# Products with v once per pair of heads, and one block fewer of the batch after next

## The chip, the cores and the metric

The kernel runs on one core of a Trainium2 chip. The metric is the device time of one execution in microseconds (us). "Faster", "same" and "slower" are said of the kernel after against the kernel before.

## What is computed

Eight batches of attention with a sigmoid in the place of the softmax, then a two-layer network over all tokens. Cut to what matters:

```python
batch, n_heads, seq, head_dim = (8, 12, 448, 64)
scores = scale * np.matmul(q, k.transpose(0, 1, 3, 2)) - np.log(S)
attn = 1.0 / (1.0 + np.exp(-scores))
x = np.matmul(attn, v)                  # -> [8*448, 768]
h = x @ w_in                            # 768 -> 2048
g = h - np.tanh(h)
out = g @ w_out                         # 2048 -> 768
```

## The kernel before

**The whole.** TensorE (PE in the profile) has by far the most work, and the order of its instructions is written out by hand: one instruction stream in which the network of batch b and the attention of later batches are interleaved. For each batch there are two stages. `moe1` computes `h` (tile `ph`, line L671) from the attention output `x`, which is split into a high and a low float16 half (`xhl`, L620 and L621), and then `g`. `moe2` computes the output: three tiles of 128 tokens (`po0` and `po1`, L789), each in 16 *steps* of 6 products, so 48 steps, and then a remainder of 64 tokens (`por`, L827), 16 shorter steps that count half. A position in a stage is thus a number from 1 to 56, and positions 16, 32 and 48 are the ends of the three tiles.

**The blocks.** Into the `moe2` stage of batch b the generator `stream` puts the attention of later batches, in *blocks*. A pair of heads takes two blocks. The first one (`i == 0`) transposes q of the next pair (`qT`, L298), the second one (`i == 1`) transposes k of the pair after (`kT`, L298 and L315). Both then compute the scores of two of the four key chunks of the pair (`sc`, L361, twelve products). ScalarE (ACT) makes the sigmoid (`a`, L370) and the high half of its result (`ahl`, L376), and VectorE (DVE) the low half (L377). These go to the list `todo`. `do_av` multiplies what the list holds with v (`acc`, L385, six products per chunk), always one block later than the scores, and with the fourth chunk the result goes out to `x` (L405, L414). In the second block of a pair ACT also reads k, q and v of a later pair for their norms (`sqn`, L307), and DVE makes the parts of k (`K`, L338 and L339).

**Where the blocks stand.** `BLOCKS0`, `BLOCKS1` and `BLOCKS` list the positions in the stages of batch 0, batch 1 and the others; this text calls them stage 0, stage 1 and so on. `ALONE` says after how many blocks of a stage the next batch is complete; what follows in the list belongs to the batch after it. Three positions after the last block that the next batch needs come its norms (`nm`, L598), and two and four positions later the rest of its `xhl`. Stage 6 runs the list only up to `ALONE`, and stage 7 has no blocks.

**Buffers.** `po0`, `po1` and `por` share two PSUM buffers (tag `mm`). At the end of a tile ACT copies `po0` out (`o`, L818) and DVE `po1` (`o`, L819); the next tile or `por` starts when its buffer is free. `qT` and `kT` share one PSUM buffer (`tr`), which `Q` and `K` on DVE set free (L339). ACT and DVE work in the order in which the program issues their instructions.

Of the kernel before, what the change touches and what calls it, by code (L numbers as in the profile page):

```python
# [34 lines left out]
class Builder:  # L35
# [6 lines left out]

    BLOCKS = (8, 12, 16, 20, 24, 28, 32, 36, 40, 44, 48, 52)
    TAIL = (1, 2, 3, 4, 5)
    ALONE = 8
    BLOCKS0 = (2, 5, 8, 12, 16, 20, 24, 31, 38)
    BLOCKS1 = (4, 7, 10, 13, 16, 19, 22, 25, 28, 32, 36, 40, 44, 48, 52)

    TP = 8
    SHIFT = 4  # L50
# [375 lines left out]
    def stream(self):  # L426

        NP = self.NP
        G = (self.B - 1) * NP
        at = lambda g: (1 + g // NP, g % NP)
        splits = lambda g: at(g)[0] >= self.AV32
        qk, v, ss, sc, K, Q, vv = {}, {}, {}, {}, {}, {}, {}

        def load(g):
            if g < G:
                qk[g] = self.load_qk(*at(g))
                if splits(g):  # L440
                    v[g] = self.load_v(*at(g), self.nat, "vn", 2)

        def norms(g):
            if g < G:
                ss[g] = self.norms(qk[g] + ([v[g]] if splits(g) else []))

        def turn(g, n, name):
            return self.transpose(qk[g][n], name) if g < G else None

        def turn_k(g):  # L450
            if g >= G:
                return None
            t = self.ps.tile([P, 512], F32, name="kT", tag="tr", bufs=1)
            turned = self.transpose(qk[g][0], "kT", t=t)
            sc[g] = self.scales(ss.pop(g), t)
            return turned

        def parts_k(g, t):
            if g < G:
                K[g] = self.parts(t, sc[g][0][:, 0:1], "K", not splits(g) and g not in (2, 3))  # L460

        def parts_q(g, t):
            if g < G:
                Q[g] = self.parts(t, sc[g][0][:, 1:2], "Q", True)
                qk.pop(g)

        def prep_v(g):
            if g >= G:
                return
            if splits(g):  # L470
                vv[g] = self.prep_v(v.pop(g), sc[g][0])
            else:
                vv[g] = self.load_v(*at(g), self.att, "vhl", 3)

        load(0)
        load(1)
        yield 0, False
        norms(0)
        norms(1)
        yield 0, False  # L480
        for g in range(2):
            parts_k(g, turn_k(g))
            yield 450, False
            parts_q(g, turn(g, 1, "qT"))
            load(g + 2)
            yield 450, False
        norms(2)
        norms(3)
        yield 0, False
        todo = []  # L490

        def do_av():
            for g, c, A in todo:
                if c == 0:
                    self.acc = self.ps.tile([P, 512], F32, name="acc", tag="av", bufs=1)
                    if g % NP == 0:
                        self.xs = []
                (self.av if splits(g) else self.av32)(c, self.acc, vv[g], A)
                if c == 3:
                    self.xs.append(self.evac_x(g % NP, self.acc, sc[g][1][:, 1:2] if splits(g) else None))  # L500
                    for d in (sc, K, Q, vv):
                        d.pop(g)
            todo.clear()

        for g in range(G):
            for i in range(2):
                if i:
                    t = turn_k(g + 2)
                elif g:
                    t = turn(g + 1, 1, "qT")  # L510
                pss = [self.scores(c, K[g], Q[g]) for c in (2 * i, 2 * i + 1)]
                aa = [self.weigh(pss[0], sc[g][1][:CK, 0:1])]
                if i:
                    parts_k(g + 2, t)
                elif g:
                    parts_q(g + 1, t)
                aa.append(self.weigh(pss[1], sc[g][1][:CK, 0:1]))
                do_av()
                if i == 0:
                    if g == 0:  # L520
                        prep_v(0)
                    prep_v(g + 1)
                if splits(g):
                    aa = [self.split_a(a) for a in aa]
                todo.extend((g, 2 * i + n, a) for n, a in enumerate(aa))
                if g and i == 0:
                    load(g + 3)
                elif g:
                    norms(g + 3)
                yield 2750, True  # L530
        do_av()
        yield 1150, True
# [344 lines left out]
    def first(self, rest):  # L877
# [17 lines left out]
        next(rest)  # L895
        assert n + len(self.BLOCKS0) + len(self.BLOCKS1) == 4 * self.NP + len(self.BLOCKS) - self.ALONE
        split = self.split_w_in()
# [14 lines left out]
    def batch(self, b):  # L912
# [12 lines left out]
        else:  # L925
            blocks = self.BLOCKS if b + 2 < self.B else self.BLOCKS[: self.ALONE + 1]
        alone = self.ALONE
        if b == 1:
            alone += len(self.BLOCKS1) - len(self.BLOCKS)
            blocks = self.BLOCKS1  # L930
        self.second(b, blocks, alone, events)
# [51 lines left out]
```

## Time and profile before

| what | us |
|---|---|
| runs of the kernel before, median of 3 | 1264.49 (1264.09 to 1266.74) |
| the profiled execution, its own time | 1264.9 |
| its span in the profile | 1262.7 |
| PE busy in it | 1234.1 |
| ScalarE busy | 933.0 |
| VectorE busy | 953.0 |

The span is what lies between the first and the last instruction; the 2.2 us beside it lie around the program. Times in rows are counted from the span's start. A row of a timeline gives the start, the length, the engine, the line, the operation, the tiles (out<-in), the shapes, the count of instructions that follow each other, and in brackets the idle time of the engine before them with what ended it.

### The profile page before, as it was taken

To read this page: it belongs to the slowest core of one execution; us is meant where nothing else is said; L and a number is where in the kernel's file an instruction comes from. 1 tells how busy PE (TensorE), PEld (TensorE's weight loads), DVE (VectorE), ACT (ScalarE), POOL (GpSimd) and SP (SyncE) were. 2 spreads that over 40 slices of the span, in tenths; PEclk is the share of its full clock that TensorE was granted. 3 is DMA by queue.
4 is the path that set the end of the run, shared out by engine and by line. 5 is a ranking of instruction groups with operands and counts; after the bars stand their busy time and mean duration, and the time that the engine had idled before them with its cause. 6 is when DMAs were issued, how large, how long until landed. Compare 5 with 4: busy or idle time off the path is not lost.

```text
span 1262.7 us, 20448 instructions
## 1 busy us (share of the span) xinstructions
PE 1234.1 (98%) x8011; PEld 683.9 (54%) x8011; DVE 953.0 (75%) x1488; ACT 933.0 (74%) x1311; POOL 37.9 (3%) x38
## 2 busy tenths in 40 slices
PE   8999879999999999999999999999999999999998
PEld 3245435555555555665555655555556655555555
DVE  4999988889876797676965798667976769645930
ACT  5967767958998688886878688886888868753820
POOL 0100000000010000100000000000000000000000
PEclk9999999999999999999999999999999999999999
DMA  9953254100122101220022200221012200100001
GB/s 258 294 139 84 58 156 138 43 27 1 36 73 57 42 2 42 65 65 7 1 57 64 56 1 16 64 58 41 1 43 67 62 7 1 28 14 20 1 13 32
DMA packets 114367, 70.52 MB, mean 56 GB/s; under 512 B 91872, under 2 KB 104416, under 8 KB 114272
## 3 DMA queue, kind: packets, MB, share of 16 engines
q1 hardware_dynamic: 114272, 69.23, 20.5%
q8 instruction: 63, 1.03, 0.3%
q14 instruction: 32, 0.26, 0.1%
HBM read 58.20 MB, written 11.01 MB: 55 GB/s over the span
## 4 chain that ended last, share of the span: by engine, by line
PE 76%; DVE 16%; ACT 4%; issue 3%; DMA 1%; SPq 0%; DVEq 0%; ACTq 0%
PE ph L671 30%; PE po L789 26%; PE sc L361 6%; PE acc L385 5%; PE por L827 3%; DVE ahl L377 2%; DVE xhl L621 2%; PE acc L395 2%; ACT a L370 1%; PE qT L298 1%; DVE sta L151 1%; DVE xhl L620 1%; DVE stb L151 1%; PE kT L298 1%; DVE wi L154 1%
## 5 line engine op out<-in xcount | busy, mean ns | idle before, releaser
L789 PE MATMUL po<-wo,g 128*128 128x384 f16 x2304 | 391.4, 326 | 1.0 <-ACT o L818 1.0
L671 PE MATMUL ph<-xhl,wi 128*128 128x448 f16 x2016 | 382.6, 352 | 0.0
L789 PEld LDWEIGHTS <-g 128*128 128x128 f16 x2304 | 219.5, 98 | 172.9 <-issue 32.4
L671 PEld LDWEIGHTS <-wi 128*128 128x128 f16 x2016 | 196.7, 98 | 185.0 <-issue 1.8
L370 ACT ACTIVATE a<-sc,nls,rn 112x896 f32<-112x896 f32 x168 | 179.7, 1094 | 45.8 <-PE sc L361 38.6
L377 DVE SCALAR_TENSOR_TENSOR ahl<-a,ahl 112x896 f16<-112x896 f32 x144 | 155.6, 1121 | 58.0 <-ACT ahl L376 57.2
L737 ACT ACTIVATE u<-ph,ih 128x896 f32<-128x896 f32 x64 | 64.4, 1006 | 99.0 <-PE ph L671 95.4
L376 ACT ACTIVATE ahl<-a 112x896 f16<-112x896 f32 x144 | 128.0, 939 | 0.0
L361 PE MATMUL sc<-Q,K 64*112 64x448 f16 x1008 | 115.2, 360 | 2.5 <-ACT a L370 2.5
L741 DVE SCALAR_TENSOR_TENSOR m<-ph,ihk,u 128x896 f32<-128x896 f32 x64 | 73.5, 1148 | 55.0 <-ACT th L739 54.7
L385 PE MATMUL acc<-ahl,vhl 112*64 112x448 f16 x864 | 96.4, 357 | 0.5
L655 ACT ACTIVATE g<-m,Sg 128x896 f16<-128x896 f32 x64 | 66.7, 1041 | 33.8 <-DVE m L755 28.7
L755 DVE COPY_PREDICATED m<-u,th 128x896 f32<-128x896 uint32 x64 | 77.1, 1205 | 6.6
L656 DVE SCALAR_TENSOR_TENSOR g<-m,Sg,g 128x896 f16<-128x896 f32 x64 | 73.4, 1147 | 8.3 <-ACT g L655 8.2
L339 DVE SCALAR_TENSOR_TENSOR Q<-qT,sn,Q 128x448 f16<-128x448 f32 x42 | 28.6, 682 | 66.8 <-ACT Q L336 66.7
L361 PEld LDWEIGHTS <-K 64*112 64x112 f16 x1008 | 59.6, 127 | 31.1 <-issue 5.2
L752 DVE SCALAR_TENSOR_TENSOR m<-q,m 128x896 f32<-128x896 f32 x64 | 69.9, 1093 | 7.4 <-DVE m L748 0.5
L701 PE MATMUL ph<-x,wi 128*128 128x448 f32 x192 | 75.1, 540 | 0.0
L742 DVE SCALAR_TENSOR_TENSOR th<-ph,ih,th 128x896 f32<-128x896 f32 x64 | 73.3, 1145 | 0.0
L754 ACT ACTIVATE u<-u,b 128x896 f32<-128x896 f32 x64 | 66.7, 1043 | 5.3 <-DVE m L741 3.3
L748 DVE SCALAR_TENSOR_TENSOR m<-q,m 128x896 f32<-128x896 f32 x64 | 69.6, 1087 | 0.0
L385 PEld LDWEIGHTS <-vhl 112*64 112x64 f16 x864 | 43.4, 109 | 47.8 <-issue 26.1
(134 smaller groups left out, 1321.7 us busy)
## 6 DMA issues: line engine op xcount, KB each, us to landing
raw<-moe_w_in SPq DMA_DIRECT2D x24, 512.0 KB, 6.0
rawo<-moe_w_out SPq DMA_DIRECT2D x32, 384.0 KB, 3.9
kn<-k SPq DMA_DIRECT2D x96, 112.0 KB, 2.9
qn<-q SPq DMA_DIRECT2D x96, 112.0 KB, 2.9
vn<-v SPq DMA_DIRECT2D x48, 224.0 KB, 2.6
out<-o SPq DMA_DIRECT2D x7, 336.0 KB, 3.3
out<-o SPq DMA_DIRECT2D x7, 288.0 KB, 3.1
out<-o SPq DMA_DIRECT2D x7, 240.0 KB, 2.6
```

The source lines that it names most:

```text
L361: nc.tensor.matmul(ps[:CK, h, :S], K[r, w, cs], Q[r, x, :], start=(n == 0), stop=(n == len(prods) - 1))
L370: nc.scalar.activation(a, ps[:CK, :, :S], AF.Sigmoid, bias=self.nls[:CK], scale=scale)
L376: nc.scalar.activation(A[:, 0], a, AF.Copy, scale=A_SCALE)
L377: nc.vector.scalar_tensor_tensor(A[:, 1], a, A_SCALE, A[:, 0], op0=ALU.mult, op1=ALU.subtract)
L385: nc.tensor.matmul(acc[h * D : (h + 1) * D, : self.S], v[:, w, h, c, :], A[:, x, h], start=(c == 0 and n == 0), stop=(c == 3 and n == 2),)
L656: nc.vector.scalar_tensor_tensor(g[:, 1], m, Sg, g[:, 0], op0=ALU.mult, op1=ALU.subtract)
L671: nc.tensor.matmul(ph[:, e, :S], self.wi[:, c * self.NB + k, part, e * P : (e + 1) * P], xhl[c][:, x, :], start=(i == 0), stop=(i == 3 * s ...
L701: nc.tensor.matmul(ph[:, e, :S], self.where("in", c)[:, f * P : (f + 1) * P], xs[c], start=(c == 0), stop=(c == self.NC - 1),)
L741: V.scalar_tensor_tensor(m, ps, ihk, u, op0=ALU.mult, op1=ALU.mult)
L742: V.scalar_tensor_tensor(th, ps, ih, th, op0=ALU.mult, op1=ALU.subtract)
L755: V.copy_predicated(m, u.bitcast(U32), th)
L789: nc.tensor.matmul(po[i][:, :H], gs[f // 2][:, x, f % 2, tk * P : (tk + 1) * P], self.wo[:, i * self.NF + f, w], start=(f == 0 and n == 0) ...
```

## The change

```diff
     TAIL = (1, 2, 3, 4, 5)
-    ALONE = 8
+    ALONE = 9
     BLOCKS0 = (2, 5, 8, 12, 16, 20, 24, 31, 38)
-    BLOCKS1 = (4, 7, 10, 13, 16, 19, 22, 25, 28, 32, 36, 40, 44, 48, 52)
+    BLOCKS1 = (4, 7, 10, 13, 16, 19, 22, 25, 28, 32, 36, 40, 46, 52)
@@ in stream
                 aa.append(self.weigh(pss[1], sc[g][1][:CK, 0:1]))
-                do_av()
+                if i == 0 or not splits(g):
+                    do_av()
```

For the pairs of batches 2 to 7 (`splits(g)`) the second block of a pair no longer multiplies with v; the first block of the next pair then does all four chunks, 24 products in place of 12. Batch 1 is as before. `ALONE` and the shorter `BLOCKS1` move one block: stage 1 has 14 blocks, not 15, and stages 2 to 5 still have 12 each, but begin one block earlier in the sequence (with the second block of pair 1, not the first of pair 2), so that every position holds the other kind of block. The last block that the next batch needs stands at position 44 there, not 40. Stage 6 has one block more. No instruction is added or left out.

On PE in stage 1, in the block at position 4 (a second block of its pair), before:

```order
L361 LDWEIGHTS K
L361 MATMUL sc<-Q,K 112x448
L385 LDWEIGHTS vhl
L385 MATMUL acc<-ahl,vhl 64x448
L385 LDWEIGHTS vhl
L385 MATMUL acc<-ahl,vhl 64x448
```

and in the changed kernel, where the line numbers below `do_av` are one higher:

```order
L361 LDWEIGHTS K
L361 MATMUL sc<-Q,K 112x448
L790 LDWEIGHTS g
L790 MATMUL po_3050<-wo,g 128x384
L790 LDWEIGHTS g
L790 MATMUL po_3051<-wo,g 128x384
```

The scores are now followed by the products of `moe2` at once; the products with v stand in the next block.

On PE at position 48 of stage 1, where the third tile ends, before:

```order
L789 MATMUL po_3889<-wo,g 128x384
L298 MATMUL qT<-ident,qn 128x112 x4
L361 LDWEIGHTS K
L361 MATMUL sc<-Q,K 112x448
L361 LDWEIGHTS K
```

and in the changed kernel:

```order
L790 MATMUL po_3888<-wo,g 128x384
L790 LDWEIGHTS g
L790 MATMUL po_3889<-wo,g 128x384
L828 LDWEIGHTS g
L828 MATMUL por<-wo,g 64x384
```

A block stood between the third tile and `por`; now `por` follows the tile directly, and the last block before it stands at position 46.

On ACT around that place the changed kernel has this order:

```order
L317 ACTIVATE tn<-kT,tiny 128x3
L370 ACTIVATE a_4153<-sc,nls,rn 112x896
L370 ACTIVATE a_4158<-sc,nls,rn 112x896
L376 ACTIVATE ahl<-a_4153 112x896
L376 ACTIVATE ahl<-a_4158 112x896
L307 ACTIVATE sqn,ss<-kn 112x512
L307 ACTIVATE sqn,ss<-qn 112x512
L307 ACTIVATE sqn,ss<-vn 112x512
L819 ACTIVATE o<-po_3888,iK 128x384
```

The copy `o` of `po0`, whose buffer `por` takes, stands behind all ACT work of the block just before it. These nine stood in the same order before, with two more steps of `moe2` between the block and the copy.

## Rows read from the trace of the kernel before

**Rows 1.** The page: busy us (share of the span) and instructions by engine.

```profile
PE 1234.1 (98%) x8011; PEld 683.9 (54%) x8011; DVE 953.0 (75%) x1488; ACT 933.0 (74%) x1311; POOL 37.9 (3%) x38
```

**Rows 2.** The timeline of PE over one block (`i == 1`) of stage 2.

```profile
493.05 0.55 PE L298 MATMUL kT<-ident,kn 112*128 112x112 f32 x4
...
493.66 1.34 PE L361 MATMUL sc<-Q,K 64*112 64x448 f16 x12
494.94 1.32 PE L385 MATMUL acc<-ahl,vhl 112*64 112x448 f16 x12
496.19 4.07 PE L789 MATMUL po<-wo,g 128*128 128x384 f16 x24
```

**Rows 3.** The chain that ended last: start, length, what; two `moe1`, batches 2 and 3.

```profile
423.91 54.59 PE ph L671 x288
...
570.94 54.59 PE ph L671 x288
```

**Rows 4.** The timeline of the end of stage 2, PE and DVE.

```profile
558.30 1.33 PE L385 MATMUL acc<-ahl,vhl 112*64 112x448 f16 x12
...
559.46 4.07 PE L827 MATMUL por<-wo,g 128*64 128x384 f16 x48
...
561.34 0.69 DVE L621 SCALAR_TENSOR_TENSOR xhl<-x,Sx,xhl 128x448 f16<-128x448 f32 x1
...
565.41 1.63 PE L385 MATMUL acc<-ahl,vhl 112*64 112x448 f16 x12
```

**Rows 5.** The timeline at the first block of stage 1 (position 4).

```profile
324.72 0.55 PE L298 MATMUL kT<-ident,kn 112*128 112x112 f32 x4
...
326.61 1.32 PE L385 MATMUL acc<-ahl,vhl 112*64 112x448 f16 x12
...
331.15 0.68 DVE L339 SCALAR_TENSOR_TENSOR K<-kT,sn,K 128x448 f16<-128x448 f32 x1
...
331.94 0.57 PE L298 MATMUL qT<-ident,qn 112*128 112x112 f32 x4 [0.98 <-ACT sqn L307]
```

**Rows 6.** The timeline at position 16 of stage 1, end of a tile.

```profile
352.17 0.60 DVE L819 TENSOR_SCALAR o<-po,iK 128x384 f32<-128x384 f32 x1
...
353.07 3.10 PE L789 MATMUL po<-wo,g 128*128 128x384 f16 x18
```

**Rows 7.** The timeline of ACT over one block (`i == 1`) of stage 1.

```profile
373.98 0.55 PE L298 MATMUL kT<-ident,kn 112*128 112x112 f32 x4
...
375.41 2.09 ACT L370 ACTIVATE a<-sc,nls,rn 112x896 f32<-112x896 f32 x2 [0.45 <-PE sc L361]
...
380.81 0.19 ACT L307 ACTIVATION_READ_ACCUMULATOR sqn<-vn 112x1 f32 x1
...
381.07 0.58 ACT L818 ACTIVATE o<-po,iK 128x384 f32<-128x384 f32 x1
```

**Rows 8.** The timeline of PE around its two longest pauses.

```profile
153.03 0.78 PE L361 MATMUL sc<-Q,K 64*112 64x448 f16 x6 [2.47 <-ACT a L370]
153.73 0.66 PE L298 MATMUL kT<-ident,kn 112*128 112x112 f32 x4
...
160.15 0.57 PE L298 MATMUL qT<-ident,qn 112*128 112x112 f32 x4 [1.17 <-ACT q L751]
161.93 1.72 PE L395 MATMUL acc<-a,vn 112*64 112x448 f32 x8
...
190.21 0.60 PE L298 MATMUL qT<-ident,qn 112*128 112x112 f32 x4 [2.19 <-DVE K L339]
190.74 1.59 PE L361 MATMUL sc<-Q,K 64*112 64x448 f16 x12
192.26 3.12 PE L395 MATMUL acc<-a,vn 112*64 112x448 f32 x8
```

**Rows 9.** Busy PE by stretch: us, busy (instructions), granted clock, DMA share, GB/s.

```profile
154.00:156.00 2.00, 2.00 (x14) 0.54 0.04 9
...
192.00:194.00 2.00, 2.00 (x8) 0.50 0.31 71
```

## The prediction

> **What bounds the kernel now.** I read the page of the profile first: PE is busy for 98% of the span [rows 1]. ACT and DVE have a quarter of the span to spare, so what counts is the time at which PE gets to each instruction, and the few places where it waits. Then I read the timeline of single blocks: how long PE spends in each piece, and what it waits for at the ends of tiles and stages. Last I listed where PE had paused for over 2 us, since a pause here has a price after it as well [rows 8, 9].
>
> **What the change saves.** In a block PE starts the twelve products with v at 494.94 and the next products of `moe2` at 496.19, so 1.25 us [rows 2]. They are six pairs that run side by side, 448 columns each; one 448-column product takes 54.59 / 288 = 0.19 us [rows 3], six take 1.14. So 0.12 is a fixed cost of each such group: it has another shape in the array than what stands before and behind it. A merged group pays it once. Where `por` follows, the fixed cost is small already: 559.46 - 558.30 = 1.16 [rows 4]. Before there are 15 groups in stage 1, 12 in each of stages 2 to 5 and 9 in stage 6, so 72, of which two a stage in stages 1 to 5 stand ahead of `por`: 62 pay. After there are 36, of which 31 pay. That saves 31 x 0.12 = 3.7 us. The trace of stages 2 to 6 has no scores followed straight by products of the full width. The nearest row: three pairs of scores at 153.03 and the transposes at 153.73 [rows 8], 0.70 for 3 x 0.19, so 0.13 for that change, the same as scores pay before the products with v (493.66 to 494.94 is 1.28, for 1.14) [rows 2]. I take it as unchanged. If it were free the saving would double, if it cost twice as much the saving would be gone: 0 to 7.4 us, and I take 3.7, since the row is of the same kind of change.
>
> **What it moves.** One block leaves stage 1 and one joins stage 6: its transposes and scores (494.94 - 493.05 = 1.89 us) and its twelve products only change place, cost 0. The block's loads on the SP queue and its work on ACT and DVE go with it. In stages 2 to 5 the norms and the last `xhl` come four positions later. Before, the last `xhl` ended at 562.03 [rows 4] and `moe1` began at 570.94 [rows 3], so 8.9 us of cover. Four positions are 4 x 0.98 us and a block, some 6 to 7. About 2 us of cover stay, and `moe1` wants its last `xhl` two thirds into its first 18 products, 2 us after it begins: cost 0, and up to 1 us a stage if DVE is later than I think.
>
> **What it costs: waits that were covered by the products with v.**
>
> 1. Position 4 of stage 1. The block begins at 324.72. PE would have been at the next transposes 0.98 us before it was: they wait until DVE has made `K`, which ends at 331.15 + 0.68 [rows 5]. DVE gets there by way of the last `g` of `moe1`, which the change doesn't touch. Without the products at 326.61 PE arrives 1.25 earlier and waits 2.2 us. The time gained is waited away, and the products come later: +1.25 in all.
>
> 2. Position 16 of stage 1. DVE's copy of `po1` ends at 352.77, PE's second product of the new tile is due at 353.07 + 0.16: 0.46 to spare [rows 6]. The block between loses 1.25. The block before is 1.14 longer, but ACT is later there too (by some 0.8, as it still has the norms of a short block to do), so DVE gains only 0.2 on PE. Wait 0.6; bounds 0 and 0.8. At positions 32 and 48 of stage 1 and at the tile ends of stages 2 to 6 the same sum leaves 0.2 to 1 us to spare.
>
> 3. Position 48 of stage 1. No block stands there now, and `por` waits for ACT's copy of `po0`. ACT first has to end the block at 46. From that block's `kT`, ACT's work ends 381.00 - 373.98 = 7.0 us later, the copy takes 0.6 [rows 7]: 7.6. PE needs 1.89 for `kT` and scores [rows 2] and 12 products of 0.163 (24 take 3.9): 3.85. So PE stands still for 3.7 us. The bounds are narrow, since both chains start at the same instruction: 3.4 to 4.
>
> 4. Stage ends. Before, the last products with v took 1.63 and not 1.33 us, as `ahl` on DVE was late [rows 4], and a few tenths more were lost around it: 0.6 a stage. In stage 1 that goes. In stages 2 to 5 a wait of much the same length takes its place: the last transposes want the buffer that `K` sets free, and `K` now stands behind two `xhl` on DVE. I take -0.6 in stage 1, -0.1 in each of stages 2 to 5, with 0.5 either way for each.
>
> Sum of the waits and the saving: -3.7 + 1.25 + 0.6 + 3.7 - 0.6 - 0.4 = **+0.8 us**. So without anything else the change would be nearly even.
>
> **The clock.** PE pauses for over 2 us twice in the trace, 2.47 us until 153.03 and 2.19 until 190.21 [rows 8]. Behind each the granted clock drops to its lower level, 1.2 GHz: 0.54 from 154 to 156, 0.50 from 192 to 194 [rows 9]. Pauses of 1.17 us [rows 8] and 0.98 us [rows 5] are followed by no such drop. The second drop shows the price: twelve scores take 1.59 and not 1.34 us [rows 8, 2], eight products with v 3.12 and not 1.72 [rows 8], so 1.65, with a few hundredths about them 1.7 us. The pauses of points 1 (2.2 us) and 3 (3.7 us) are as long as these or longer. Before, neither was there. Work behind both is PE's own, with nothing that it would wait for anyway, so I add 1.7 twice: 0.8 + 3.4 = **+4.2 us**. The bounds are 0 and 3.4.
>
> The Trainium skill (TensorE: Matmul & The Clock Gate, "HAM oscillation") warns of pauses longer than the two of rows 8; by that rule only the pause of point 3 would lower the clock, and the sum would be 2.5. Rows 8 and 9 speak against the rule as it stands, and they decide.
>
> **The rivals.**
>
> *One drop only.* The pause at position 4 is at the edge of what rows 8 show, 2.2 us against 2.19, and may lower the clock in some executions and not in others. Then 0.8 + 1.7 = +2.5: 1267.0. For it: the nearest row that dropped is the shorter one. Against: both long pauses did.
>
> *No drop.* The clock stays up, as after 0.98 and 1.17 us. Then +0.8: 1265.3, no change. Against it: the pause of point 3 is half as long again as the longest that dropped.
>
> *The waits don't come.* Faster: the saving of 3.7 and the 0.6 of stage 1 stay, with 0.4 from stages 2 to 5, and points 1 to 3 cost nothing: 1264.5 - 4.7 = 1259.8. It decides at `por`: if ACT has the copy of `po0` done within 3.85 us of that `kT`, there's no pause. For it: ACT is idle for a quarter of the span [rows 1]. Against it: ACT's order there has two sigmoids, two halves and three norms ahead of the copy, 5.6 us of work [rows 7]. The change not doing what it says isn't open: the order of PE's instructions shows it.
>
> *ACT falls behind in the short blocks.* Slower still: a short block lasts 1.89 us and its steps, in stage 1 4.8 us, and ACT has 5.6 us of work in it. I let the longer block make up for it. If it doesn't, each pair loses some 0.3 us in stage 1 and 0.1 elsewhere, about 5 us: 1273.5. It decides where `K` or the first sigmoid of a block ends after PE wants its buffer; I find 1 us to spare in most blocks, 0.15 at position 12 of stages 2 to 6.
>
> **How the numbers follow.** The profiled execution took 1264.9 us, 0.4 above the median of the three runs; +4.2 gives 1269.1 against it and 1268.7 against the median, 1264.5. The chances: both drops 0.42, one drop 0.22, none 0.13, no waits 0.12, ACT behind 0.11. Two in a thousand of the time are 2.5 us, about what a measurement of this kernel can tell from no change. The first and the last case are slower by more than that, the second is on the line (0.12 over it, 0.10 within), the third within, the fourth faster: slower 0.65, same 0.23, faster 0.12. The range goes from the case with no drop, less 0.9 for the sizes in points 2 and 4 (1264.4), to the forecast plus 2 (1270.7). It leaves out the faster case and the farther half of the last.
>
> **What would show it.** Right: `por` of stage 1 waits some 3.7 us for ACT's `o`; the second transposes of stage 1 wait 2.2 us and not 1; the windows behind both show a clock of 0.5; the period from one `moe1` to the next in stages 2 to 5 is 0.7 us shorter (147.0 before, [rows 3]), and stage 1 is longer although it has a block less. Wrong: the clock stays at 1 behind one or both, `moe1` of some batch waits for `xhl`, or scores followed by `moe2` cost something else than 0.13.

## The result and the profile after

The changed kernel took 1269.65 us (median of 12 runs, 1266.64 to 1271.87); the kernel before took 1265.1 (12 runs, 1263.99 to 1268.31). The ratio is 1.0031, 95% interval 1.0023 to 1.004: slower by some 4 us. The profiled execution is the slowest of the twelve, 1271.87 us by its own time with a span of 1269.7. Its work is that of before:

```profile
PE 1234.2 (97%) x8011; PEld 685.9 (54%) x8011; DVE 953.4 (75%) x1488; ACT 934.2 (74%) x1311; POOL 37.9 (3%) x38
```

PE is as busy as in [rows 1]. Time at a lower clock counts as busy too, so this row can't show what was saved and what was lost. To see where time went, one divides the span at the starts of `moe1`. The chain of waits of the changed kernel, for the two batches of [rows 3] (start, length, what):

```profile
431.22 54.59 PE ph L672 x288
...
577.53 54.59 PE ph L672 x288
```

Between the two lie 146.31 us, before 570.94 - 423.91 = 147.03. The same subtraction for every stage, of this kernel and of the experiments below, against the kernel before (stage b runs from `moe1` of batch b to the next; all from such chain rows):

| kernel | stage 1 | stages 2 to 5 | stage 6 | sum, against before | ratio of the runs |
|---|---|---|---|---|---|
| before | 157.51 | 588.11 | 134.90 | | |
| after | 161.94 | 585.26 | 137.45 | +4.13 | 1.0031 |
| e1 | 157.59 | 585.27 | 137.44 | -0.22 | 0.9994 |
| e2 | 158.99 | 585.27 | 137.44 | +1.18 | 1.0010 |
| e3 | 155.05 | 585.26 | 137.45 | -2.76 | 0.9981 |
| e4 | 158.62 | 585.26 | 137.45 | +0.81 | 1.0006 |
| e5 | 156.46 | 586.87 | 138.05 | +0.86 | 1.0011 |
| e6 | 160.08 | 583.81 | 134.41 | -2.22 | 0.9977 |
| e7 | 158.31 | 585.27 | 137.44 | +0.50 | 0.9997 |
| e8 | 152.60 | 585.27 | 137.44 | -5.21 | 0.9961 |
| e9 | 156.27 | 583.80 | 134.41 | -6.04 | 0.9948 |

The spans of the two profiles differ by 7.0 us, these stages by 4.13. The other 2.9 lie ahead of `moe1` of batch 1, which begins between 265.6 and 269.3 us in the eleven profiled executions, with or without the change; they don't belong to it (the merging begins with batch 2, whose blocks stand in stage 1). So stage 1 lost 4.43 us with a block less, stages 2 to 5 won 0.71 each, and stage 6 paid 2.55 for its block.

The timeline of PE in the changed kernel at position 4 of stage 1, to be read beside [rows 5]:

```profile
327.60 0.55 PE L298 MATMUL kT<-ident,kn 112*128 112x112 f32 x4
328.21 1.34 PE L361 MATMUL sc<-Q,K 64*112 64x448 f16 x12
329.49 3.10 PE L790 MATMUL po<-wo,g 128*128 128x384 f16 x18
334.83 0.57 PE L298 MATMUL qT<-ident,qn 112*128 112x112 f32 x4 [2.25 <-ACT sqn L307]
335.34 2.10 PE L361 MATMUL sc<-Q,K 64*112 64x448 f16 x12
337.37 3.34 PE L385 MATMUL acc<-ahl,vhl 112*64 112x448 f16 x24
```

The scores are followed by `moe2` at once, PE comes to the transposes earlier, and 0.98 us of waiting has become 2.25. Behind it twelve scores take 2.10 and not 1.34 us. The bracket names a norm of ACT; what ended the wait is the second half of `K`, as the timeline of DVE shows:

```profile
334.05 0.68 DVE L339 SCALAR_TENSOR_TENSOR K<-kT,sn,K 128x448 f16<-128x448 f32 x1
```

It ends at 334.73, 7.13 us behind the start of `kT`; in [rows 5] these are 331.83 and 7.11 us. DVE is as late as it was, PE is earlier.

At position 48, PE and then ACT:

```profile
410.42 1.34 PE L361 MATMUL sc<-Q,K 64*112 64x448 f16 x12
411.69 2.12 PE L790 MATMUL po<-wo,g 128*128 128x384 f16 x12
417.35 5.77 PE L828 MATMUL por<-wo,g 128*64 128x384 f16 x48 [3.53 <-ACT o L819]
```

```profile
411.24 2.09 ACT L370 ACTIVATE a<-sc,nls,rn 112x896 f32<-112x896 f32 x2 [0.45 <-PE sc L361]
413.21 1.78 ACT L376 ACTIVATE ahl<-a 112x896 f16<-112x896 f32 x2
414.89 0.62 ACT L307 ACTIVATE sqn<-kn 112x512 bf16<-112x512 f32 x1
...
416.73 0.57 ACT L819 ACTIVATE o<-po,iK 128x384 f32<-128x384 f32 x1
```

ACT never idles between the sigmoids at 411.24 and the copy `o`, which ends at 417.30; `por` starts 0.05 later. And 48 products of `por` take 5.77 us where [rows 4] have 4.07. The windows say why (us from and to, length, busy PE and its instructions, granted clock, DMA share, GB/s):

```profile
332.00:335.00 3.00, 0.75 (x6) 1.00 0.00 0
336.00:339.00 3.00, 3.00 (x18) 0.50 0.34 77
413.00:417.00 4.00, 0.82 (x6) 1.00 0.07 15
418.00:421.00 3.00, 3.00 (x22) 0.50 0.00 0
```

Through both pauses the granted clock is still at its upper level, 2.4 GHz; behind each it is at 0.50, which is 1.2 GHz. Both are new: in the trace of before no such window lies in stage 1.

The end of stage 2 in the changed kernel, beside [rows 4]:

```profile
568.61 0.68 DVE L339 SCALAR_TENSOR_TENSOR K<-kT,sn,K 128x448 f16<-128x448 f32 x1
...
569.39 0.57 PE L298 MATMUL qT<-ident,qn 112*128 112x112 f32 x4 [0.34 <-issue]
...
574.95 0.69 DVE L622 SCALAR_TENSOR_TENSOR xhl<-x,Sx,xhl 128x448 f16<-128x448 f32 x1
...
577.46 2.82 PE L672 MATMUL ph<-xhl,wi 128*128 128x448 f16 x14
```

The last transposes wait 0.34 us, until 0.10 us behind the end of `K` (569.29), as at position 4, and the last `xhl` of the next batch ends at 575.64, 1.8 us ahead of its `moe1`.

### The profile page after: what moved, and what is told of

It is laid out like the page before. It is cut to its first block, busy times and chain, and to the rows that moved or that the text cites. A ratio compares the mean times of both kernels' runs of the same rounds, so it can differ in the third digit from the quotient of the medians.

```text
span 1269.7 us, 20400 instructions
## 1 busy us (share of the span) xinstructions
PE 1234.2 (97%) x8011; PEld 685.9 (54%) x8011; DVE 953.4 (75%) x1488; ACT 934.2 (74%) x1311; POOL 37.9 (3%) x38
## 4 chain that ended last, share of the span: by engine, by line
PE 81%; DVE 9%; ACT 4%; issue 3%; DMA 2%; SPq 0%; DVEq 0%; ACTq 0%
PE ph L672 30%; PE po L790 27%; PE sc L361 7%; PE acc L385 7%; PE por L828 5%; DVE stb L151 1%; DMA raw<-moe_w_in 1%; PE acc L395 1%; PE qT L298 1%; PE kT L298 1%; ACT a L370 1%; ACT sqn L307 1%; DVE stb L150 1%; DVE m L742 1%; DVE m L753 1%
## 5 line engine op out<-in xcount | busy, mean ns | idle before, releaser
L385 PE MATMUL acc<-ahl,vhl 112*64 112x448 f16 x864 | 89.5, 357 | 0.0
L828 PE MATMUL por<-wo,g 128*64 128x384 f16 x768 | 66.5, 332 | 4.6 <-ACT o L819 4.6
```

Source lines behind the costliest of these rows:

```text
L385: nc.tensor.matmul(acc[h * D : (h + 1) * D, : self.S], v[:, w, h, c, :], A[:, x, h], start=(c == 0 and n == 0), stop=(c == 3 and n == 2),)
L828: nc.tensor.matmul(po[e * D : (e + 1) * D, :H], gs[f // 2][:, x, f % 2, nm:S], self.wo[:, e * self.NF + f, w], start=(f == 0 and n == 0), ...
```

## The experiments

The theory under test: each half of the change is cheap or good, and the loss comes from two pauses of PE in stage 1, each paid once as waiting and once more as a lower clock behind it. Rival A: the clock is a bystander, and the waiting itself or other work accounts for the loss. Rival B: ACT and DVE are behind everywhere, so that a wait that is mended comes back elsewhere. All ratios are against the kernel before, on the same chip; the edits are to the changed kernel unless said otherwise.

**e1: the last block before the remainder back to position 48.**

```diff
-    BLOCKS1 = (..., 32, 36, 40, 46, 52)
+    BLOCKS1 = (..., 32, 36, 40, 48, 52)
```

> One position is changed in the changed kernel: the block of stage 1 at 46 goes to 48, so that it stands between the third tile and por again. Theory (two pauses and two drops of the clock): the pause of 3.5 us before por goes, and with it the 1.7 us of the lower clock behind it; 1269.65 - 5.2 = 1264.4, a ratio to the kernel before of 0.9995. The pause of 2.25 us at the second block and its drop stay. Rival A (a pause costs only its own length, the clock plays no part): 1269.65 - 3.5 = 1266.1, ratio 1.0008. Rival B (ACT falls behind in the short blocks, in all stages): hardly less than 1269, ratio 1.003.

Measured: 0.9994 (0.9985 to 1.0004). One number in a table takes the whole loss away. The timeline of PE there:

```profile
409.89 4.09 PE L828 MATMUL por<-wo,g 128*64 128x384 f16 x48
415.03 0.57 PE L298 MATMUL qT<-ident,qn 112*128 112x112 f32 x4 [1.04 <-ACT sqn L307]
```

`por` doesn't wait any more; the transposes at 52, with less between them and the block before, wait 1.04 us for `K` instead, which DVE ends at 414.93:

```profile
414.25 0.68 DVE L339 SCALAR_TENSOR_TENSOR K<-kT,sn,K 128x448 f16<-128x448 f32 x1
```

So the pause at `por` was worth 3.53 + 1.7 - 1.04 = 4.2 us; stage 1 is 4.35 shorter.

**e2: the blocks behind position 4 later.**

```diff
-    BLOCKS1 = (4, 7, 10, 13, 16, ...)
+    BLOCKS1 = (4, 9, 11, 14, 16, ...)
```

> In the changed kernel the second block of stage 1 goes from position 7 to 9, the two behind it from 10 to 11 and from 13 to 14; all others stay. PE has two more steps of moe2, 1.96 us, before the transposes that wait for K. Theory: the pause of 2.25 us shrinks to 0.3, no drop of the clock follows; the pause before por stays: 1269.65 - 1.95 - 1.7 = 1266.0, ratio 1.0007. Rival A (no price of the clock): 1267.7, ratio 1.0021. Rival B (ACT behind in short blocks): no better than 1269, and a wait appears at the blocks that moved closer together.

Measured: 1.0010 (0.9999 to 1.0020). The wait at the second block falls to 0.31 us and no lower clock follows. But at position 16 a wait grew:

```profile
350.79 2.34 DVE L377 SCALAR_TENSOR_TENSOR ahl<-a,ahl 112x896 f16<-112x896 f32 x2 [1.10 <-ACT ahl L376]
353.06 0.61 DVE L820 TENSOR_SCALAR o<-po,iK 128x384 f32<-128x384 f32 x1
...
353.71 2.60 PE L790 MATMUL po<-wo,g 128*128 128x384 f16 x15 [1.28 <-DVE o L820]
```

In the changed kernel it was 0.33. With blocks at 14 and 16, DVE's copy of the tile stands behind the work of the block at 14: what holds up `por` (a copy queued behind a block), at another tile and on another engine. At `por` the lower clock cost less than before, 48 products in 5.41 us and not 5.77:

```profile
413.03 5.41 PE L828 MATMUL por<-wo,g 128*64 128x384 f16 x48 [3.54 <-ACT o L819]
```

Its windows show a clock of 0.67 from 412 to 413 us, so the level fell while PE still waited. Together: 1.94 of the wait at the second block, some 1.7 of the clock behind it and 0.36 at `por` are won, 0.95 is lost at position 16; that makes 3.05, and stage 1 is 2.95 shorter.

**e3: both, e1 and e2.**

> Both moves at once. Theory: neither long pause, no drop of the clock in stage 1: 1269.65 - 5.2 - 3.65 = 1260.8, ratio 0.9966, and what is left is the saving of some 0.12 us in each merged group. Rival A: 1264.1 (0.9992). Rival B: near 1269 (1.003).

Measured: 0.9981 (0.9971 to 0.9991). Faster than before, yet by 2.4 us and not by the expected 4.3. The waits of 1.28 (position 16) and 1.05 us (position 52) are both there. No pause of over 2 us and no lower clock are left in stage 1, so rival B has a part: mending a wait by moving a block opened a smaller one, twice.

**e4: the two pauses filled with unneeded products.** Nothing of the schedule is changed; nine products of a constant tile stand ahead of the second block of stage 1, and fifteen ahead of `por`, so that PE works while it would wait. `left` counts the blocks of stage 1 and reaches 0 at the second one; the lines of this kernel are numbered 7 to 9 higher (L305 here is L298).

```diff
+        if b == 1:
+            self.fill(15)
...
+            if left[0] == 0:
+                self.fill(9)
```

> The changed kernel, with products that nobody needs in both pauses of stage 1: nine of 128x512 (some 1.95 us) ahead of the second block, fifteen (some 3.2 us) ahead of por. The schedule and the waits stay as they are: por and the transposes start when they did. Theory: the clock doesn't drop behind either, and only that is gained: 1269.65 - 3.4 = 1266.2, ratio 1.0008. Rival A (the clock plays no part in the loss): 1269.6, ratio 1.0031. If only the longer pause lowered the clock in most executions: 1268, ratio 1.0018.

Measured: 1.0006 (0.9996 to 1.0016). The timeline of PE and the windows of this run:

```profile
330.04 2.11 PE L96 MATMUL fill<-onesb 128*128 128x512 bf16 x9
332.45 0.57 PE L305 MATMUL qT<-ident,qn 112*128 112x112 f32 x4 [0.31 <-issue]
...
409.63 3.40 PE L96 MATMUL fill<-onesb 128*128 128x512 bf16 x15
413.33 4.09 PE L837 MATMUL por<-wo,g 128*64 128x384 f16 x48 [0.30 <-ACT o L826]
```

```profile
333.00:336.00 3.00, 3.00 (x33) 1.00 0.21 48
...
413.00:416.00 3.00, 2.70 (x35) 1.00 0.02 5
```

The needed work starts no sooner (the transposes 7.23 us behind the block's `kT` at 325.22, in the changed kernel 334.83 - 327.60 = 7.23; `por` 6.94 us behind the scores of the block at 46, which began at 406.39, there 417.35 - 410.42 = 6.93), and the clock stays up behind both places: 48 products of `por` take 4.09 us and not 5.77. Stage 1 is 161.94 - 158.62 = 3.32 us shorter with 24 products more. This is the clock's price alone, two times 1.66, and rival A falls: of the 4.1 us that the change costs, the clock has 3.3.

**e5: the moved block alone.** `do_av` in every block again, the positions of the changed kernel.

```diff
-                if i == 0 or not splits(g):
-                    do_av()
+                do_av()
```

> The changed kernel with the products with v in both blocks of a pair again: the new positions alone, no merging. Theory: the second block of stage 1 waits 1.0 us as before, with no drop of the clock; por of stage 1 waits for ACT's copy, 3.5 less the 1.25 us that PE now spends on twelve products in the block at 46, so 2.3 us, and the clock drops behind it in some executions (1.7 us, taken as 1). Sum against the kernel before: 2.3 + 1 - 0.6 of old waits in stage 1 - 0.2 in each of stages 2 to 5: +1.9, ratio 1.0015. Rival (the loss of the change is in the merging, the new positions are free): ratio 1.000 or below, and por doesn't wait.

Measured: 1.0011 (1.0001 to 1.0020).

```profile
408.42 2.12 PE L789 MATMUL po<-wo,g 128*128 128x384 f16 x12
412.82 4.09 PE L827 MATMUL por<-wo,g 128*64 128x384 f16 x48 [2.28 <-ACT o L818]
```

```profile
413.00:416.00 3.00, 3.00 (x40) 1.00 0.02 5
```

The wait at `por` is there without the merging, 2.28 us; the products with v in the block at 46 cover the other 1.25 (3.53 - 2.28). So the rival of this run (the new positions are free, `por` doesn't wait) falls. In this execution no lower clock follows a pause of 2.28 us.

**e6: the merging alone.** The kernel before with its positions and `ALONE`; the second blocks of a pair don't multiply with v, but for one pair of each batch.

```diff
-                do_av()
+                if i == 0 or not splits(g) or g % NP == 1:
+                    do_av()
```

> The kernel before, its positions and ALONE, with the merging alone; only pair 1 of each batch, whose second block ends a stage, still multiplies in both blocks, so that no more halves are held over a stage's end than before. Theory: 30 groups fewer, 0.12 us each: -3.6; the second block of stage 1 waits 2.25 and not 1.0 us: +1.25, with a drop of the clock in some executions, taken as +1.0; the copy at position 16 +0.3; por isn't held up, as a block stands at 48; a wait of 0.4 for K at 48 in each of five stages: +2. Sum +1.0, ratio 1.0008, with a spread of 1 us either way from the drops. Rival (merging saves nothing, the array's change of shape is paid anyway): +4.5, ratio 1.0035.

Measured: 0.9977 (0.9968 to 0.9986): faster by 2.9 us, where a slight loss was expected. The timeline of PE at position 4 of stage 1 and at 48 of stage 2:

```profile
332.65 0.57 PE L298 MATMUL qT<-ident,qn 112*128 112x112 f32 x4 [2.26 <-ACT sqn L307]
...
559.65 2.46 PE L385 MATMUL acc<-ahl,vhl 112*64 112x448 f16 x24
561.95 4.07 PE L828 MATMUL por<-wo,g 128*64 128x384 f16 x48
```

The pause at position 4 is the expected one, with the lower clock behind it. But in stages 2 to 5 there is no wait at all, neither at `por` nor at the end of the stage, where the kernel before lost some half a microsecond (1.07 less five savings of 0.12): each of these stages is 1.07 us shorter than before, and 0.36 shorter than in the changed kernel. The expectation missed because it put waits where the order of before leaves none.

**e7: position 44 in the place of 46.**

```diff
-    BLOCKS1 = (..., 32, 36, 40, 46, 52)
+    BLOCKS1 = (..., 32, 36, 40, 44, 52)
```

> The changed kernel with the block of stage 1 at 44 in place of 46: two more steps of moe2 between it and por, 1.96 us, and still no block at 48. Theory: por waits 3.53 - 1.96 = 1.6 us, too short for the clock to drop (1.2 us never was enough, 2.2 at times): 1269.65 - 1.96 - 1.7 = 1266.0, ratio 1.0002 to 1.0008. Rival (a pause costs its own length alone): 1267.7, ratio 1.002. Rival (any pause of over 1.5 us drops the clock): the same 1267.7, with 0.5 in the records behind por.

Measured: 0.9997 (0.9988 to 1.0006).

```profile
413.08 4.09 PE L828 MATMUL por<-wo,g 128*64 128x384 f16 x48 [1.58 <-ACT o L819]
```

```profile
413.00:416.00 3.00, 2.92 (x36) 1.00 0.00 0
```

Two steps (1.96 us) earlier, the pause is 1.95 us shorter, and the clock stays up behind 1.58 us. Stage 1 is 3.63 us shorter: 1.95 of waiting and 1.68 of clock, nearly twice what the wait alone shows.

**e8: all blocks of stage 1 spread anew**, so that no copy stands right behind a block and none follows its forerunner too closely.

```diff
-    BLOCKS1 = (4, 7, 10, 13, 16, 19, 22, 25, 28, 32, 36, 40, 46, 52)
+    BLOCKS1 = (4, 9, 12, 16, 18, 21, 23, 26, 28, 32, 35, 40, 44, 48)
```

> The changed kernel with the list of stage 1 drawn up anew from what the runs showed: 4, 9, 12, 16, 18, 21, 23, 26, 28, 32, 35, 40, 44, 48. The second block comes late enough for K; the tile ends at 16 and 32 have blocks with 24 products with v, which cover the copies; 48 has a block, so por is covered; nothing stands at 52. Theory: of the 1.28 us (copy at 16) and the 1.05 us (last transposes) that PE waits in e3_both, 1.3 and 0.6 go: 1263.7 - 1.9 = 1261.8, ratio 0.9966. Rival (ACT can't follow where only two steps lie behind a long block): a new wait at 18, 23, 28 or 35, and no gain over e3_both (0.998).

Measured: 0.9961 (0.9949 to 0.9973), 1261.36 us against the 1261.8 expected. In stage 1 one wait of over 0.2 us is left, 0.31:

```profile
334.39 0.57 PE L298 MATMUL qT<-ident,qn 112*128 112x112 f32 x4 [0.31 <-issue]
```

So rival B holds only for the positions tried in e2 and e3: ACT and DVE do have the time, if the blocks are placed for them.

**e9: e6 with the positions of e8 and the fifteenth block at 52.**

```diff
-    BLOCKS1 = (4, 7, 10, 13, 16, 19, 22, 25, 28, 32, 36, 40, 44, 48, 52)
+    BLOCKS1 = (4, 9, 12, 16, 18, 21, 23, 26, 28, 32, 35, 40, 44, 48, 52)
```

> The merge alone (twelve blocks of before in place, none moved to stage 6), with the positions of stage 1 spread as in e8 and the fifteenth block still at 52. Theory: the merge saves time wherever its second block does not run into the chain of the block ahead, so of the merge alone (0.9977) only the pause of 2.26 us at position 4, the one of 0.68 at position 16 and one lower clock (1.7 us) are left to win: 1.95 + 0.68 + 1.7 = 4.3 us, ratio 0.9943, stage 1 some 155.8 us long and stages 2 to 5 some 145.95. Rival A: moving the blocks to stage 6 has a gain of its own, and e8 (0.9961) is better than this. Rival B: with fifteen blocks the spread positions open a wait at another place, 0.9965 or more, and the trace shows a pause of over 1 us in stage 1.

Measured: 0.9948 (0.9934 to 0.9961), 1259.31 us: the fastest of all, 10 us under the changed kernel by the medians (the kernel before took 1265.43 us beside this run and 1265.1 beside the changed kernel). Its chain of waits:

```profile
425.06 54.59 PE ph L672 x288
...
571.01 54.59 PE ph L672 x288
```

The period is 145.95 us, as in e6, and stage 1 took 156.27 for the 155.8 expected. Rival A of this run wanted e8 to be the better one; it isn't, though the intervals of the two overlap, so no gain of moving the block to stage 6 is seen. Rival B falls: the longest wait of PE left in stage 1 is 0.41 us.

## Why the prediction was right

Forecast +4.2 us and 1268.7; measured 1269.65, and +4.13 in the stages of the profile. The two parts of the forecast come out as well: +0.8 without the clock, where e4, which takes the clock away, has +0.81 in the table; and 3.4 for the clock, where e4 wins 3.32. Step by step:

- **The saving (0.12 per merged group).** Right. In the changed kernel 24 products with v and the step to `moe2` take 558.79 - 556.40:

```profile
556.40 2.46 PE L385 MATMUL acc<-ahl,vhl 112*64 112x448 f16 x24
558.79 3.10 PE L790 MATMUL po<-wo,g 128*128 128x384 f16 x18
```

  2.39 us, for two times 1.25 in [rows 2]: 0.11. Stage 6, which has no stage end, gives 138.05 (e5) - 137.45 = 0.60 for five pairs, so 0.12.

- **Scores followed by `moe2`, the cost that no row of before showed.** Right: from 328.21 to 329.49 are 1.28 us, and [rows 2] have the same 1.28 from scores to products with v. Of the bounds 0 and 7.4 for the saving, 3.7 was the place.

- **Point 1, position 4.** Right: a wait of 2.25 for 2.2. **Point 3, `por`.** Right: 3.53 for 3.7; the two chains started at the same `kT`, and both could be added up from [rows 2, 7].

- **Point 2, position 16.** The mechanism was right, the size too large: 0.33 for 0.6, inside the bounds 0 to 0.8. Timeline of DVE and PE:

```profile
357.37 0.61 DVE L820 TENSOR_SCALAR o<-po,iK 128x384 f32<-128x384 f32 x1
...
358.03 2.92 PE L790 MATMUL po<-wo,g 128*128 128x384 f16 x17 [0.33 <-DVE o L820]
```

- **Point 4, stage ends.** Right: the period of stages 2 to 5 is 0.71 us shorter for 0.7, and the new wait for `K` is 0.34 us. The cover of `xhl` is 1.8 us for "about 2". The 0.6 won at the end of stage 1 was too much. The timeline of PE before shows one late group there:

```profile
418.38 1.62 PE L385 MATMUL acc<-ahl,vhl 112*64 112x448 f16 x12
419.82 4.09 PE L827 MATMUL por<-wo,g 128*64 128x384 f16 x48
```

  1.44 us where a group ahead of `por` takes 1.16 [rows 4], so 0.28. The sizes of points 2 and 3 were too large by 0.27 and 0.17, this gain by some 0.3, and the errors cancel. That the sum of 0.8 fits to within a tenth is luck; that each term is there is not.

- **The clock.** The step that decided, and right in size: two lower clocks, 3.32 us in e4 for 3.4. The ground it stood on was weaker than it looked. Two rows of one execution (a pause of 2.47 and one of 2.19 us, both followed by a lower clock) were taken for what such pauses always do. That one execution held both was luck: only the kernel before and e3, two of eleven executions, show a lower clock behind both pauses of over 2 us in [rows 8]. Over the eleven profiled executions of this study, from 140 us on:

| pause of PE | length, us | how often | lower clock behind it |
|---|---|---|---|
| first of [rows 8] | 2.47 | 11 | 7 |
| the next, where the first had no lower clock | 2.73 | 4 | 0 |
| last of [rows 8] | 2.19 | 11 | 4 |
| position 4 of stage 1 | 2.25 | 4 | 4 |
| `por` of stage 1 (e5) | 2.28 | 1 | 0 |
| `por` of stage 1 (after, e2) | 3.53 | 2 | 2 |
| any of 1.6 and less | | many | 0 |

A fall counts here when it begins between 0.7 us ahead of the pause's end and 1.6 us behind it.

Between 2.1 and 2.8 us the clock fell in 15 of 31 cases, and length doesn't order them: 2.73 never, 2.25 each time. What does, beyond length, these runs leave open. So "one drop only" deserved more than its 0.22: pauses near 2.2 us lower the clock in some executions and not in others. The time of the changed kernel goes with its clock from run to run: in its four runs under 1268 us the mean granted clock is 0.995 to 0.996, in the eight above 1269 it is 0.992 to 0.995, and one fall that costs 1.7 us takes 0.0013 from it. A mean doesn't say at which pauses the runs differ. That the two pauses of the change pay in most runs is shown by e4 against all runs: 1.0031 - 1.0006 is 3.2 us of the 3.4, and the mean granted clock of all runs, 0.9942 against 0.9966 in e4, says 3 us.

The Trainium skill (TensorE: Matmul & The Clock Gate, "HAM oscillation") warns of longer pauses than the one at position 4. The trace does not agree with it there: 2.25 us lowered the clock in four executions of four.

**What the sum did not see.** It was made for both halves at once, and by the runs they are not two small losses: the merging alone gains 2.9 us (e6, which merges five pairs of six), the moved block alone costs 1.4 (e5), and together they should gain 1.5, not lose 3.9. The 5.4 us between are in two places by the profiled executions. In stage 1 (2.9 us by the table) the merging takes 1.25 us of cover from the block at 46, so that the pause at `por` grows from 2.28 to 3.53 us and gets the lower clock (1.7): 2.95. In stages 2 to 5 (2.7 us) each half alone ends the late finish of the stage (0.31 us in e5, some 0.47 in e6), which can be won only once, and together they make the wait of 0.34 for `K`: 0.31 + 0.34 = 0.65 in each of four stages, 2.6. This second split is worked out from the table; no run takes the wait for `K` alone away.

## What to carry to other kernels

Where instructions that filled a gap are moved away, look for what the gap was long enough for: a wait that grows past some 2 us on TensorE can cost its length and 1.7 us again (in these runs at times from 2.19 us on, never at 1.58). A copy that frees a buffer must not be queued on ACT or DVE right behind a block's work, and a block's position should be chosen by the engine that then has the most to do, not by even spacing (e8). Time the halves of a change apart: here one half alone was a gain, and a new list of positions for stage 1 (e9) more than doubled that gain.

## What the hardware showed that was not expected

The lower clock does not follow from the length of a pause alone in this range (the table above), and behind the same first pause of [rows 8] it lasted 3.4 us in two of the executions (the kernel before, e1) and 6.8 in five; the windows of the changed kernel show it, from 155 to 161.5 us and gone behind 162:

```profile
155.00:158.00 3.00, 2.97 (x16) 0.50 0.00 0
158.00:161.50 3.50, 3.50 (x18) 0.50 0.29 66
162.00:165.00 3.00, 2.76 (x24) 1.00 0.05 12
```

Filling a pause with unneeded products (e4) keeps the clock and costs nothing where PE waits anyway: 24 products, 3.3 us won.
